# Hash attention and a SwiGLU block on one core: first loads by way of a landing room, key signs spread before the last sum, bits first in each pair's first score tile

## The chip, the core and the metric

The kernel runs on one NeuronCore of a Trainium2 chip. The engines named below work side by side and meet only at semaphores: TensorE multiplies matrices into PSUM (PE in the profile; PEld is its weight load), VectorE (DVE) and ScalarE (ACT) do elementwise work, GpSimd (POOL) sets constants and issues some DMAs, and SyncE (SP) issues most of the DMAs. ScalarE, too, issues a few at the start. Each has a queue of its own. The metric is the device time of one execution in microseconds, lower is better.

## What is computed

Attention over 4 batches, 8 heads, 768 positions and 64 features, in which a query sees only the keys with the same hash bucket, and then a SwiGLU block over the 3072 x 512 result. Cut to what matters:

```python
q_bits = (np.einsum('bhsd,dk->bhsk', q, proj) > 0)      # 6 signs for each query
k_bits = (np.einsum('bhsd,dk->bhsk', k, proj) > 0)
q_bucket = np.sum(q_bits * powers, axis=-1)             # k_bucket likewise
mask = q_bucket[:, :, :, None] == k_bucket[:, :, None, :]
scores = np.where(mask, scale * np.matmul(q, k.transpose(0, 1, 3, 2)), -1000000000.0)
attn = softmax(scores)                                  # with 1e-09 in the denominator
x = np.matmul(attn, v)                                  # -> (B*S, H*D)
g = x @ w_gate
out = (g * sigmoid(g) * (x @ w_val)) @ w_out
```

## The kernel before

**Stages.** `attention` goes through 16 pairs of heads (`pairs`, numbered 0 to 15 here), and `gated_block` then runs the SwiGLU block. Between the two, and beside both, the weights are taken apart into three parts each ("pieces": `begin_pieces` on ScalarE, `advance_pieces` with `widths` and `parts` on VectorE, loads and stores on GpSimd's queue), and attention results are split the same way (`split`, L287 to L296).

**One pair.** A pair has 12 score tiles ("units" u): two halves of 384 queries by six chunks of 128 keys, each tile for both heads. `score(u)` makes two products into the same PSUM tile: `products` multiplies transposed keys and queries in f32 (`T`) and starts the accumulation, and `mark` adds the product of the sign bits in bf16 (`bits`), which lifts matching buckets by a large number, and then has ScalarE take the exponential into a ring of weight tiles `A` (L530). After the 12 tiles, `attend` multiplies the weights with v (`av`, L545), 48 matmul records, about 7.9 us.

**Sums.** While the tiles are made, `add` sums their weights on VectorE: L563 at i = 3 and 9, L567 and L570 at i = 5 and 11. `total(n-1)` has TensorE sum the previous pair's accumulators over the partitions (L581), ScalarE copies the row out of PSUM (`fetch_row`, L586), SP moves it into `few`, VectorE inverts it (`invert`, L594), SP sends it through DRAM and back spread over the partitions, and `norm` (L610) scales the result.

**The next pair's front.** `front(n+1)` gives three steps, of which two transpose k and q on VectorE (`transpose_blocks`, L458) and stand at the head of pair n, and the third, `hash_next`, comes after the 12 tiles: four hash products (L430), then the signs of q on ScalarE (L435), the copy of the q bits to the other 32 partitions by a GpSimd DMA (`spread_q`, L447), and, handed back as a list, the signs of k and `spread_k` on VectorE (L444), which multiplies the key signs for each head. The list is worked off by `finish(rest)` after the row copy and after the last `add`.

**Order.** All order is written out by hand: `manual_schedule` leaves each engine the order of the program text. Raw k and q have one buffer each, so `load(n + 2, "qk")` on SP waits until pair n+1 is transposed. `few` stands on SP behind these eight loads.

**The start.** Pair 0 has its own path. Its q comes on SP's queue and its k on ScalarE's, in halves and by heads, four DMAs for each tensor, straight into the raw tiles [128, 6, 2, 64] (L329), so that a run of memory is 64 numbers long. `start_first` transposes them on TensorE (`tps`, L468), ScalarE evicts k (L472) and VectorE q (L475); then come the first products, the hash of all four halves, their signs and spreads, and three tiles. Ahead of it TensorE runs nine matmuls over zeros (`idle`, L367), and `hash_w` is filled from `proj` by two VectorE copies (L394).

Of the kernel before, what the change touches and what calls it, by code (L numbers as in the profile page):

```python
# [19 lines left out]
def kernel(  # L20
# [68 lines left out]
    def finish(todo):  # L89
        while todo:  # L90
            todo.pop(0)()
# [210 lines left out]
    def attention(scope):  # L302
# [9 lines left out]
        def fetch(n, name, queue, half=None):  # L312
            b, pr = pairs[n]
            if name == "v":
                t = raws["v", n] = raw.tile([P, 2, NCH, D], FP32, tag="vraw", name="vraw")
                queue.dma_start(
                    t.rearrange("p h c d -> p h (c d)"),
                    v[b, 2 * pr : 2 * pr + 2].rearrange("h (p c) d -> p h (c d)", c=NCH),
                )
                return  # L320
            src = q if name == "q" else k
            if not half:
                raws[name, n] = raw.tile([P, NCH, 2, D], FP32, tag=name + "raw", name=name + "raw",
                                         bufs=1)
            t = raws[name, n]
            if n == 0:
                cs = slice(half * CH, (half + 1) * CH)
                for h in range(2):
                    queue.dma_start(t[:, cs, h, :],  # L329
                                    src[b, 2 * pr + h].rearrange("(p c) d -> p c d", c=NCH)[:, cs, :])  # L330
                return
            blocks = t.rearrange("p c a b -> p (c a b)").rearrange(
                "p (c a d) -> p c a d", a=P // BLOCK, d=BLOCK)
            for h in range(2):
                for x in range(D // BLOCK):
                    at = h * D + x * BLOCK
                    queue.dma_start(
                        blocks[at : at + BLOCK],
                        src[b, 2 * pr + h][:, x * BLOCK : (x + 1) * BLOCK].rearrange(
                            "(a p c) d -> p c a d", c=NCH, p=BLOCK))  # L340

        def load(n, names):
            if n < len(pairs):
                for name in names:
                    fetch(n, name, nc.sync)

        two_proj = fixed.tile([P, NBITS], FP32, tag="proj", name="proj")
        for o in (0, D):
            nc.gpsimd.dma_start(two_proj[o : o + D, :], proj[:, :])
# [13 lines left out]
        for t in (sides["k", 0], sides["q", 0], sides["q", 1]):  # L363
            nc.vector.memset(t, 0.0)
        idle = two_banks("idle")
        for i in range(9):
            nc.tensor.matmul(idle[:, i % 2], zeros[:, 0:P], zeros[:, 0:512], start=True, stop=True)  # L367

        HR = 16
# [19 lines left out]

        hash_w = fixed.tile([P, BLOCK], FP32, tag="hash", name="hash")  # L390
        nc.vector.memset(hash_w, 0.0)
        for h in range(2):
            rows = slice(h * D, (h + 1) * D)
            nc.vector.tensor_copy(hash_w[rows, h * HR : h * HR + NBITS], two_proj[rows, :])  # L394
        ones = fixed.tile([P, BLOCK], FP32, tag="ones", name="ones")
        nc.gpsimd.memset(ones, 1.0)

# [5 lines left out]
            nc.gpsimd.memset(t.rearrange("p u h q -> p (u h) q")[:, :, HQ:AW], 1.0)  # L403
            twos.append(t)
        ring = [t[:, i] for t in twos for i in range(2)]

        for n, name in ((1, "k"), (1, "q"), (0, "v"), (1, "v")):
            fetch(n, name, nc.sync)
        load_words(3, nc.sync)

        T = {}
        bits = {}
# [9 lines left out]
        def front(n):  # L422
# [24 lines left out]
                nc.gpsimd.dma_start(bits["q", n][high], bits["q", n][low])  # L447

            def hash_next(todo):
                q0, q1, *ks = hash_blocks(todo)  # L450
                q0()
                q1()
                spread_q()
                return ks + [lambda: spread_k(times_k)]

            def transpose_blocks(name):
                T[name, n] = opnd.tile([P, S], FP32, tag=name + "T", name=name + "T")
                nc.vector.transpose(T[name, n], raws[name, n].rearrange("p c h d -> p (c h d)"))  # L458

            def start_first():  # L460
                for half in range(2):
                    cols = slice(half * HQ, (half + 1) * HQ)
                    for name in "kq":
# [7 lines left out]
                        if name == "k":  # L471
                            nc.scalar.activation(T[name, n][:, cols], ps[:, 0:HQ], AF.Copy,  # L472
                                                 scale=2 / OFF)
                        else:
                            nc.vector.tensor_copy(T[name, n][:, cols], ps[:, 0:HQ])  # L475

                def both_heads(sign, name, half):
                    cols = slice(half * HQ, (half + 1) * HQ)
# [33 lines left out]

        banks_of = {}

        def product(u, x, start):
            n, half, c = units[u]
            qs = slice(half * HQ, (half + 1) * HQ)
            ks = slice(c * P, (c + 1) * P)
            for h in range(2):
                rows = slice(h * D, (h + 1) * D)  # L520
                nc.tensor.matmul(banks_of[u][:, h], x["k", n][rows, ks], x["q", n][rows, qs],  # L521
                                 start=start, stop=not start)

        def products(u):
            banks_of[u] = two_banks("sc")[:, :, 0:HQ]
            product(u, T, True)

        def mark(u):
            product(u, bits, False)
            nc.scalar.activation(weights(u)[:, :, 0:HQ], banks_of.pop(u), AF.Exp,  # L530
                                 scale=SCALE * (1.0 if units[u][0] else OFF / 2))

        def score(u):
            products(u)
            mark(u)

        def attend(u):
            n, half, c = units[u]
# [84 lines left out]
                    rest.extend(f for f in steps.pop(0)() or [] if f)  # L623

        front(0)
        steps = front(1)
        last = []
        PACE = [2] * 4 + [1] * 4 + [2, 1] * 4
# [3 lines left out]
        for n in range(len(pairs)):  # L632
# [5 lines left out]
            for i in range(2 * NCH):  # L638
                if u + i > 2:
                    score(u + i)  # L640
                if n == 0 and i == TURN:
                    prepare_pair(2)
                if i % NCH:
                    add(u + i)
                if i == (2 if n else TURN):
                    load(n + 2, "qk")
            row = total(n - 1) if n else None
            if more:
                prepare_pair(1)
            if row:  # L650
                row()
            finish(rest)
            finish(last)
            while waiting:
                last.append(waiting.pop(0)())
# [277 lines left out]
```

## Time and profile before

| what | us |
|---|---|
| median of 3 runs (lowest, highest) | 913.04 (912.83, 913.85) |
| the profiled execution, device time | 913.47 |
| its span, first to last instruction | 911.4 |
| TensorE busy, attention and block | 904.0 |
| first full stream of score matmuls begins | 13.33 |
| attention's last matmul ends, block begins | 318.5 |
| one pair, score tiles to score tiles, from pair 1 on | 19.23 |

The span counts from the first to the last instruction of the program; the device time has 2.1 us more around it. A line of a timeline or of the chain in order of time starts with its start and its length in microseconds; several instructions of one kind that follow each other are merged (x4). "[0.58 <-PE joint L430]" says how long the engine had been idle before it, and what ended that. SPq, POOL DMA and ACTq lines are DMA issues, and not the transfers themselves. A chain of waits is followed backward from the last instruction: to what released it, or to the instruction before it on the same engine.

### The profile page before, as it was taken

Reading aid. Unit: us, or ns where it says so; the run is one execution under the profiler, and the core shown is the slowest. Engines: PE = TensorE matmul, PEld = TensorE weight load, DVE = VectorE, ACT = ScalarE, POOL = GpSimd, SP = SyncE. Lnnn points to the kernel's source line nnn. Section 1 sums busy time; section 2 is a strip of 40 time slices with the busy share of each in tenths; the row PEclk is TensorE's granted clock in tenths of the full one; section 3 lists DMA queues with packets and bytes.
Section 4 is the critical chain, followed back from the end, with each engine's and each line's share of the span. In section 5 each row is a group of like instructions: output and inputs, shape, how many; then the busy total and the mean of one; then the engine's idle time right before and its main releaser. Section 6 shows DMA issues by size and latency. Waiting matters only on the chain.

```text
span 911.4 us, 12610 instructions
## 1 busy us (share of the span) xinstructions
PE 904.0 (99%) x4795; PEld 636.1 (70%) x4795; DVE 666.6 (73%) x774; ACT 448.0 (49%) x604; POOL 97.0 (11%) x193
## 2 busy tenths in 40 slices
PE   8999999999999999999999999999999999999998
PEld 4444444444444488888888888888888888888886
DVE  5889999989988968779785855465668754474746
ACT  6889888878888655452414243331313233413220
POOL 1111111011111120000100000101000100001000
PEclk9999999999999999999999999999999999999999
DMA  7777788787897599685756562444434642525332
GB/s 180 132 188 199 195 214 192 162 193 208 224 227 211 200 382 331 218 289 207 297 177 238 202 259 104 173 139 157 155 139 151 242 147 97 207 70 208 104 139 93
DMA packets 145579, 174.25 MB, mean 191 GB/s; under 512 B 106496, under 2 KB 115200, under 8 KB 145520
## 3 DMA queue, kind: packets, MB, share of 16 engines
q0 software_dynamic: 22864, 116.36, 36.4%
q1 hardware_dynamic: 121056, 56.71, 24.9%
q8 instruction: 38, 0.62, 0.3%
q10 hardware_dynamic: 1600, 0.39, 0.2%
q14 instruction: 21, 0.17, 0.1%
HBM read 133.17 MB, written 39.42 MB: 189 GB/s over the span
## 4 chain that ended last, share of the span: by engine, by line
PE 97%; DVE 1%; DMA 1%; ACTq 0%; issue 0%; ACT 0%; DVEq 0%
PE a L690 29%; PE o L690 22%; PE sc L521 17%; PE n L690 14%; PE av L545 13%; PE joint L581 1%; PE joint L430 1%; DMA vraw<-in_v_dram 1%; DMA kraw<-in_k_dram 0%; DVE both L567 0%; DVE both L563 0%; DVE acc L570 0%; ACTq L329 0%; DVE kb L444 0%; DVE kT L458 0%
## 5 line engine op out<-in xcount | busy, mean ns | idle before, releaser
L690 PE MATMUL a<-xparts,ring 128*128 128x512 f32 x1152 | 273.0, 389 | 0.0
L690 PEld LDWEIGHTS a<-xparts,ring 128*128 128x128 f32 x1152 | 216.1, 188 | 45.5 <-issue 0.6
L690 PE MATMUL o<-ring,hid 128*128 128x512 f32 (+1 forms) x870 | 199.1, 388 | 0.0
L690 PEld LDWEIGHTS o<-ring,hid 128*128 128x128 f32 x870 | 162.1, 188 | 35.2 <-DVE hid L745 1.0
L521 PE MATMUL sc<-qT,kT 64*128 64x384 f32 x768 | 156.9, 487 | 0.6 <-ACT A L530 0.6
L530 ACT ACTIVATE A<-sc 128x768 f32<-128x768 f32 x192 | 151.8, 815 | 7.5 <-PE sc L521 4.2
L690 PE MATMUL n<-xparts,ring 128*128 128x512 f32 x576 | 142.2, 389 | 0.0
L545 PE MATMUL av<-A,vraw 128*64 128x386 f32 (+1 forms) x768 | 127.7, 488 | 0.0
L690 PEld LDWEIGHTS n<-xparts,ring 128*128 128x128 f32 x576 | 108.1, 188 | 22.5
L735 DVE TENSOR_TENSOR v<-v,n 128x1024 f32<-128x1024 f32 x36 | 44.0, 1221 | 98.7 <-PE n L690 98.0
L248 POOL DMA_DIRECT2D ring<-ram x108 | 56.9, 529 | 499.9 <-PE n L690 328.4
L545 PEld LDWEIGHTS av<-A,vraw 128*64 128x64 f32 x768 | 53.7, 136 | 73.3 <-issue 63.4
L521 PEld LDWEIGHTS sc<-qT,kT 64*128 64x128 f32 x768 | 67.6, 187 | 48.5 <-issue 46.3
L729 ACT ACTIVATE g<-a 128x1024 f32<-128x1024 f32 x36 | 37.0, 1027 | 130.8 <-PE a L690 126.6
L740 ACT ACTIVATE hid<-v 128x1024 fp32r<-128x1024 f32 x36 | 38.2, 1062 | 114.5 <-DVE v L739 114.5
L737 ACT ACTIVATE g<-g 128x1024 f32<-128x1024 f32 x36 | 38.2, 1062 | 86.0 <-DVE g L735 86.0
L792 DVE TENSOR_TENSOR o<-o 128x512 f32<-128x512 f32 x92 | 63.0, 687 | 20.6 <-ACT o L786 18.2
L735 DVE TENSOR_TENSOR g<-g,n 128x1024 f32<-128x1024 f32 x36 | 43.8, 1217 | 32.7 <-PE n L690 32.7
L521 PE MATMUL sc<-qb,kb 64*128 64x384 bf16 x384 | 63.4, 323 | 1.1 <-DVE kb L444 1.1
L567 DVE TENSOR_TENSOR both<-both,A 128x1536 f32<-128x1536 f32 x32 | 56.2, 1757 | 3.2
L563 DVE SCALAR_TENSOR_TENSOR both<-A 128x1536 f32<-128x1536 f32 x32 | 55.7, 1741 | 3.5 <-ACT A L530 1.9
L743 DVE SCALAR_TENSOR_TENSOR hid<-hid,v 128x1024 fp32r<-128x1024 f32 x36 | 44.0, 1224 | 19.2 <-ACT hid L740 19.1
(79 smaller groups left out, 696.8 us busy)
## 6 DMA issues: line engine op xcount, KB each, us to landing
ring<-ram POOLq DMA_DIRECT2D x108, 768.0 KB, 5.1
ram<-stage POOLq DMA_DIRECT2D x23, 768.0 KB, 5.6
ram<-stage SPq DMA_DIRECT2D x13, 768.0 KB
qraw<-in_q_dram SPq DMA_DIRECT2D x64, 96.0 KB
vraw<-in_v_dram SPq DMA_DIRECT2D x16, 384.0 KB
out_dram<-o SPq DMA_DIRECT2D x23, 256.0 KB
kraw<-in_k_dram SPq DMA_DIRECT2D x60, 96.0 KB
r<-sums SPq DMA_DIRECT2D x30, 192.0 KB
```

Of the source, the lines that this page charges most:

```text
L248: nc.gpsimd.dma_start(t.bitcast(FP32), ram[at].bitcast(FP32))
L521: nc.tensor.matmul(banks_of[u][:, h], x["k", n][rows, ks], x["q", n][rows, qs], start=start, stop=not start)
L530: nc.scalar.activation(weights(u)[:, :, 0:HQ], banks_of.pop(u), AF.Exp, scale=SCALE * (1.0 if units[u][0] else OFF / 2))
L545: nc.tensor.matmul(ps[h * D : (h + 1) * D, 0:width], raws["v", n][:, h, c, :], a[:, h, 0:width], start=c == 0, stop=c == NCH - 1)
L563: nc.vector.scalar_tensor_tensor(out=t, in0=first, scalar=S * EPS / P / 2, in1=now, op0=ALU.add, op1=ALU.add)
L567: nc.vector.tensor_tensor(t, t, now, op=ALU.add)
L690: nc.tensor.matmul(ps, w, x, start=start, stop=stop)
L735: nc.vector.tensor_tensor(two(z), two(z), n_, op=ALU.subtract)
L737: nc.scalar.activation(z, z, AF.Silu)
L740: nc.scalar.activation(h, val, AF.Copy, scale=TOWARD / STEP)
L743: nc.vector.scalar_tensor_tensor(out=l, in0=h.bitcast(FP32), scalar=-STEP, in1=val, op0=ALU.mult, op1=ALU.add)
L792: nc.vector.tensor_tensor(accs[c], accs[c], t[:, 1], op=ALU.subtract)
```

## The change

The first pair's k and q no longer land in the raw tiles. A room with the shape of the tile `both` (same buffer) takes each tensor in the order of memory, [128, head, 6, 64]; a DMA now brings one half of one tensor for both heads, in runs of 192 numbers. `start_first` begins with four copies into the raw tiles, k on ScalarE and q on VectorE, first half and second half, ahead of every eviction. One idle matmul is dropped, the filling of `hash_w` moves behind the first half's evictions, and the loads of pair 1's k and q, of two v tiles and of three weight pieces move, in the text, behind `front(0)`.

In every pair, `hash_next` hands back all six steps, the signs of k and their spread first, then the signs of q and their copy. Three of them run ahead of the last `add`, which is taken out of the loop; the others follow it, and the row copy follows all of them.

`score` makes the bits product first in each pair's first tile (u a multiple of 12), and the f32 product closes the accumulation; in all other tiles the order stays.

```diff
@@ -324,10 +324,10 @@
                                          bufs=1)
             t = raws[name, n]
             if n == 0:
-                cs = slice(half * CH, (half + 1) * CH)
-                for h in range(2):
-                    queue.dma_start(t[:, cs, h, :],
-                                    src[b, 2 * pr + h].rearrange("(p c) d -> p c d", c=NCH)[:, cs, :])
+                at = slice(half * CH * D, (half + 1) * CH * D)
+                queue.dma_start(
+                    landing[name].rearrange("p h c d -> p h (c d)")[:, :, at],
+                    src[b, 2 * pr : 2 * pr + 2].rearrange("h (p c) d -> p h (c d)", c=NCH)[:, :, at])
                 return
             blocks = t.rearrange("p c a b -> p (c a b)").rearrange(
                 "p (c a d) -> p c a d", a=P // BLOCK, d=BLOCK)
@@ -344,6 +344,9 @@
                 for name in names:
                     fetch(n, name, nc.sync)
 
+        room = att.tile([P, 2, 2, HQ], FP32, tag="both", name="landing", bufs=1)
+        landing = {name: room[:, i].rearrange("p x q -> p (x q)").rearrange(
+            "p (h c d) -> p h c d", h=2, d=D) for i, name in enumerate("qk")}
         two_proj = fixed.tile([P, NBITS], FP32, tag="proj", name="proj")
         for o in (0, D):
             nc.gpsimd.dma_start(two_proj[o : o + D, :], proj[:, :])
@@ -363,7 +366,7 @@
         for t in (sides["k", 0], sides["q", 0], sides["q", 1]):
             nc.vector.memset(t, 0.0)
         idle = two_banks("idle")
-        for i in range(9):
+        for i in range(8):
             nc.tensor.matmul(idle[:, i % 2], zeros[:, 0:P], zeros[:, 0:512], start=True, stop=True)
 
         HR = 16
@@ -389,9 +392,6 @@
 
         hash_w = fixed.tile([P, BLOCK], FP32, tag="hash", name="hash")
         nc.vector.memset(hash_w, 0.0)
-        for h in range(2):
-            rows = slice(h * D, (h + 1) * D)
-            nc.vector.tensor_copy(hash_w[rows, h * HR : h * HR + NBITS], two_proj[rows, :])
         ones = fixed.tile([P, BLOCK], FP32, tag="ones", name="ones")
         nc.gpsimd.memset(ones, 1.0)
 
@@ -404,10 +404,6 @@
             twos.append(t)
         ring = [t[:, i] for t in twos for i in range(2)]
 
-        for n, name in ((1, "k"), (1, "q"), (0, "v"), (1, "v")):
-            fetch(n, name, nc.sync)
-        load_words(3, nc.sync)
-
         T = {}
         bits = {}
 
@@ -447,17 +443,19 @@
                 nc.gpsimd.dma_start(bits["q", n][high], bits["q", n][low])
 
             def hash_next(todo):
-                q0, q1, *ks = hash_blocks(todo)
-                q0()
-                q1()
-                spread_q()
-                return ks + [lambda: spread_k(times_k)]
+                q0, q1, k0, k1 = hash_blocks(todo)
+                return [k0, k1, lambda: spread_k(times_k), q0, q1, spread_q]
 
             def transpose_blocks(name):
                 T[name, n] = opnd.tile([P, S], FP32, tag=name + "T", name=name + "T")
                 nc.vector.transpose(T[name, n], raws[name, n].rearrange("p c h d -> p (c h d)"))
 
             def start_first():
+                for half in range(2):
+                    here = slice(half * CH, (half + 1) * CH)
+                    for name, copy in (("k", nc.scalar.copy), ("q", nc.vector.tensor_copy)):
+                        copy(raws[name, n].rearrange("p c h d -> p h c d")[:, :, here],
+                             landing[name][:, :, here])
                 for half in range(2):
                     cols = slice(half * HQ, (half + 1) * HQ)
                     for name in "kq":
@@ -473,6 +471,11 @@
                                                  scale=2 / OFF)
                         else:
                             nc.vector.tensor_copy(T[name, n][:, cols], ps[:, 0:HQ])
+                    if not half:
+                        for h in range(2):
+                            rows = slice(h * D, (h + 1) * D)
+                            nc.vector.tensor_copy(hash_w[rows, h * HR : h * HR + NBITS],
+                                                  two_proj[rows, :])
 
                 def both_heads(sign, name, half):
                     cols = slice(half * HQ, (half + 1) * HQ)
@@ -512,27 +515,34 @@
 
         banks_of = {}
 
-        def product(u, x, start):
+        def product(u, x, start, stop):
             n, half, c = units[u]
             qs = slice(half * HQ, (half + 1) * HQ)
             ks = slice(c * P, (c + 1) * P)
             for h in range(2):
                 rows = slice(h * D, (h + 1) * D)
                 nc.tensor.matmul(banks_of[u][:, h], x["k", n][rows, ks], x["q", n][rows, qs],
-                                 start=start, stop=not start)
+                                 start=start, stop=stop)
 
         def products(u):
             banks_of[u] = two_banks("sc")[:, :, 0:HQ]
-            product(u, T, True)
-
-        def mark(u):
-            product(u, bits, False)
+            product(u, T, True, False)
+
+        def mark(u, last=True):
+            if last:
+                product(u, bits, False, True)
             nc.scalar.activation(weights(u)[:, :, 0:HQ], banks_of.pop(u), AF.Exp,
                                  scale=SCALE * (1.0 if units[u][0] else OFF / 2))
 
         def score(u):
-            products(u)
-            mark(u)
+            if u % (2 * NCH):
+                products(u)
+                mark(u)
+            else:
+                banks_of[u] = two_banks("sc")[:, :, 0:HQ]
+                product(u, bits, True, False)
+                product(u, T, False, True)
+                mark(u, False)
 
         def attend(u):
             n, half, c = units[u]
@@ -623,6 +633,9 @@
                     rest.extend(f for f in steps.pop(0)() or [] if f)
 
         front(0)
+        for n, name in ((1, "k"), (1, "q"), (0, "v"), (1, "v")):
+            fetch(n, name, nc.sync)
+        load_words(3, nc.sync)
         steps = front(1)
         last = []
         PACE = [2] * 4 + [1] * 4 + [2, 1] * 4
@@ -640,16 +653,20 @@
                     score(u + i)
                 if n == 0 and i == TURN:
                     prepare_pair(2)
-                if i % NCH:
+                if i % NCH and i < 2 * NCH - 1:
                     add(u + i)
                 if i == (2 if n else TURN):
                     load(n + 2, "qk")
             row = total(n - 1) if n else None
             if more:
                 prepare_pair(1)
+            for _ in range(3):
+                if rest:
+                    rest.pop(0)()
+            add(u + 2 * NCH - 1)
+            finish(rest)
             if row:
                 row()
-            finish(rest)
             finish(last)
             while waiting:
                 last.append(waiting.pop(0)())
```

## The prediction

> **What bounds the kernel now.** I read the page's busy line, then the chain of waits, then the chain in order of time for the first 125 us.
>
> ```profile
> PE 904.0 (99%) x4795; PEld 636.1 (70%) x4795; DVE 666.6 (73%) x774; ACT 448.0 (49%) x604; POOL 97.0 (11%) x193
> ...
> PE 97%; DVE 1%; DMA 1%; ACTq 0%; issue 0%; ACT 0%; DVEq 0%
> ```
>
> TensorE sets the end, and its matmuls are not made fewer. Only three things can be won: the start, stalls, and bubbles between stages. The chain in order of time shows the first two:
>
> ```profile
> 2.37 4.12 DMA kraw<-in_k_dram
> 6.49 0.14 issue
> 6.62 0.85 PE tps L468 x6
> 7.47 0.84 PE sc L521 x4
> 8.32 0.78 PE joint L430 x8
> ...
> 13.33 6.88 PE sc L521 x50
> ...
> 106.50 0.42 DVE kb L444
> 106.94 0.42 DVE kb L444
> 107.36 0.14 issue
> 107.50 9.22 PE sc L521 x68
> ```
>
> The start waits for the last landing of k, at 2.37 + 4.12 = 6.49; from there to the hash (8.25 in the timeline) is 1.76, and from 13.33 on TensorE runs through. At 107.50 it waited for key signs (kb, L444) that VectorE reached late. The timelines of single engines show the rest:
>
> ```profile
> 28.83 0.92 PE L521 MATMUL sc<-qT,kT 64*128 64x384 f32 x4
> 29.58 0.33 PE L521 MATMUL sc<-qb,kb 64*128 64x384 bf16 x2
> 29.74 0.81 PE L521 MATMUL sc<-qT,kT 64*128 64x384 f32 x4
> ...
> 40.29 1.16 ACT L435 ACTIVATE qb<-joint,columns 32x384 bf16<-32x384 f32 x2 [0.58 <-PE joint L430]
> 41.47 0.48 ACT L586 COPY row<-joint 128x384 f32<-128x384 f32 x1
> 41.97 1.18 ACT L435 ACTIVATE kb<-joint,columns 32x384 bf16<-32x384 f32 x2
> ...
> 45.20 0.23 DVE L594 RECIPROCAL few<-few 128x12 f32<-128x12 f32 x1 [1.17 <-DMA few<-row]
> ...
> 96.18 0.93 DVE L458 STREAM_TRANSPOSE qT<-qraw 128x768 f32<-128x768 f32 x1
> ...
> 119.66 0.52 POOL L447 DMA_DIRECT2D qb<-qb  x1 [3.62 <-ACT qb L435]
> ```
>
> The first f32 product after the attention stage takes 0.92, the next 0.81: a bubble of 0.11. The rows of 40 to 45 are a second loop: row copy, `few` out on SP, reciprocal, weight pieces, the next pair's transposes, SP's loads, `few` again. The transposes end at 53.56, 74.88, 97.11 and 116.42; the hashes that need them start at 58.62, 77.85, 97.16 and 117.3. So this loop is slower than TensorE up to the fourth pair, catches it at 97.16, and is left behind again afterwards. What it gains or loses in pair 1 arrives at TensorE there.
>
> **The start.** Eight loads with 256-byte runs become four with 768-byte runs. The windows of 2 to 6 us show the DMA engines 0.85, 1.16, 1.09 and 0.76 busy, so packets set the landing. By the trace's packet records 256 bytes take 18 ns and 1024 bytes 46 ns; on that line 768 bytes take 37. Before: 3072 x 18 / 16 = 3.5 us, really 1.86 to 5.85. After: 1024 x 37 / 16 = 2.4 us, with the same slack 2.7, so 1.86 to 4.6, plus 0.4 to 0.6 to the semaphore: the second halves land at 5.0 (bounds 4.7 to 5.6, where issue or receipt holds them).
>
> Added are four copies. ScalarE: 128x384 as L472, 0.49. VectorE: between 0.35 (L153 does 512 elements out of SBUF in 0.42) and 0.56 (L475, out of PSUM); 0.35 taken, and it doesn't decide. The first k copy runs about 4.0 to 4.5, so transposes start near 4.75. The first eviction on ScalarE queues behind the second k copy (5.02 to 5.51) and runs to 6.0; the second transposes start at 5.65 and end by 6.25; products run 6.44 to 7.29. `hash_w`'s two copies (0.17 each) now stand behind the first q eviction on VectorE (5.65 to 6.2), so the second q eviction runs 6.6 to 7.16, just ahead of the hash at 7.29. **Start: -0.95**, bounds -0.35 and -1.25. The path beyond the hash is unchanged. The moved loads keep their order on SP, where none of the start's instructions stands among them; their first waited for the k transposes (issue at 7.18) and comes with these. The landing room is needed again at 15.60 (L563), ten us later.
>
> One idle matmul less: they start 0.43 apart (nine from 1.32, 4.00 us), so eight end by 4.9 and nothing waits for the ninth. Against this speaks the Trainium skill, "TensorE: Matmul & The Clock Gate", "What's actually happening": the clock is released after a busy window of about 3.4 us that is not tied to the kernel's start. Eight times 0.43 is 3.4, no margin. By the rows the sum keeps -0.95; by the rule a missed window leaves products and hash (0.84 + 0.78) at half rate, up to +1.6. One case in ten, as transposes follow at once.
>
> **The row copy moves back.** On ScalarE the order q, q, row, k, k becomes k, k, q, q, row. In pair 1 `few` leaves at 41.97, right behind the row. New: 41.97 - 0.95 - 0.10 (bits first, below) + 1.16 = 42.08. It landed 3.2 later there; in the next pairs issue to reciprocal is 2.2 (64.31 to 66.51, 84.91 to 87.09). I take 2.2: reciprocal at 44.28 instead of 45.20, **-0.92**; with 3.2 again it is +0.1. VectorE is no earlier: its L563 of 38.12 ends at 38.84 shifted, it then waits for the k signs until 40.43 (cover gone, 1.6 idle), spreads (0.85), sums (1.76 + 0.96) and is free at 44.1. In pair 2 that wait is under 0.4 and lies inside the 1.79 idle before 66.51. From pair 3 on VectorE comes later than the signs, and spread ahead of sum costs it nothing. In later pairs `few` stands behind SP's k loads (81.62 + 3.19, then 84.91), so the later row is hidden.
>
> **Pair 4.** Transposes end at 97.11 - 0.92 = 96.19, hash at 96.24. TensorE alone would be there at 97.08 - 0.95 - 4 x 0.10 = 95.7, so 0.5 of the gain is lost in this wait. **Key signs ahead of the sum:** the spread of 106.50 moves in front of L567 and L570 (103.64 to 106.46), 2.8 us; the first bits product was due 0.75 after its scores began (105.85), at 106.60, and came at 107.50: **-0.90**. What is late next is pair 5's hash: 117.32 - 0.92 - 0.90 - 0.10 = 115.40, while its transposes come at 116.42 - 0.92 = 115.50. So -1.77 there.
>
> **Query bits come later.** Behind the k signs the POOL copy of q bits starts 1.16 later, and bits first needs it 0.75 sooner. The trace's issue to landing is 2.1 to 5.3, median 3.6. From its start the attention stage leaves 7.91; issue stands at 1.58, now 2.74, so 5.17 is allowed. Only pair 5 (119.66, 5.3) exceeds it: +0.15. POOL's following transfers wait for VectorE anyway.
>
> **Bits first.** The f32 product's bubble of 0.11 falls away; a bits product after a wait shows 0.34 against 0.33, so 0.01 remains: 0.10 per pair. The same page's section "LDWEIGHTS (loading the stationary operand)" prices a load by columns alone, 128 / 1.2 = 107 ns whatever the type; by that the swap would bring nothing but the fast load for non-f32 weights, about 0.05. The row decides: weight loads of 64x128 are 187 ns in f32, 93 in bf16. Fifteen pairs have such a tile; the first five are already in the sums above, the ten from pair 6 on give **-1.0** (by the rule -0.5).
>
> **Sum.** -1.77 + 0.15 - 1.0 = -2.6 on the profiled execution (913.47, span 911.4): 910.9. The median of the runs shown is 913.04, and part of these 0.43 may be the 3.2 us landing, which other executions need not share; without it the kernel before gains by itself. I therefore add 0.2: **911.1**.
>
> **Rivals.**
> - *The loop eats the start* (0.25). The `few` landing stays at 3.2, or second halves land at 5.6: -2.6 + 0.6 to 1.0, and against a median without that landing about -1.3: 911.5 to 912.2. For it: the reciprocal waits 1.17 for `few` in the trace. Against: 2.2 in the pairs after.
> - *Query bits late in every pair* (0.12), the slower side. If 1.16 later puts the copy into SP's loads each time, as at 99.53 (4.9) and 119.66 (5.3), TensorE stops at the first tile of each pair. It decides from a landing of 5.17 on; at 5.7, 0.5 x 14 = 7 us, less 2.6: 917. Against: twelve of fifteen take 4.3 or less.
> - *The clock comes a window later* (0.08): +1.0 to 1.6, 912 to 912.5.
> - *More than forecast* (0.10): landing at 4.7 and no wait at 96.2: 909.6 to 910.2.
> - The forecast itself, 910.3 to 911.6: 0.45.
>
> A difference under 0.2% (1.83 us, 911.21 to 914.87) can't be told from none. Faster: 0.40 of the forecast's 0.45, all of the 0.10, 0.06 of the loop's: 0.56. Slower: 0.12, and 0.01 for what I overlook. Within: 0.31. The range 909.6 to 913.0 covers all but the slower case and some of the tail.
>
> **What would show it.** k's second half lands near 5.0 and TensorE runs through from about 12.4; the reciprocal of pair 1 stands near 44.3; the wait for kb at 107.5 is gone; VectorE idles 1.6 ahead of the first spreads only; the first f32 product after attention reads 0.81, fifteen times. Wrong would be: waits on q bits at several pair starts, a hash near 97.2 or later, or a start above 13.

## The result and the profile after

| what | before | after |
|---|---|---|
| median of 13 runs each, us (lowest, highest) | 912.75 (912.07, 913.85) | 911.12 (910.13, 911.90) |
| the profiled execution, device time | 913.47 | 910.18 |
| its span | 911.4 | 908.4 |
| first hash of the start (the L430 product of 8.25, now L426) | 8.25 | 7.46 |
| reciprocal of pair 1 | 45.20 | 44.29 |
| hash of pair 4 | 97.16 | 95.91 |
| hash of pair 5 | 117.32 | 115.14 |
| attention's last matmul ends, block begins | 318.49 | 315.31 |
| one pair, score tiles to score tiles (most pairs) | 19.23 | 19.13 |

The hash of pair 4 is the one behind pair 4's score tiles; it makes the signs for pair 5, so a wait for these shows at pair 5's first tile. Three pairs of before were longer than the others: 19.34 (pair 4), 20.13 (pair 5) and 19.31 (pair 6). After the change only pair 5 is, with 19.26.

Changed over unchanged time is 0.9982, with a 95% interval of 0.9973 to 0.9990: 1.6 us less. The same kernel run again beside the experiments (e4 below) gave 910.58 against 913.08, 0.9975 (0.9966 to 0.9985), 2.5 us less. The profiled execution of before was near the top of that kernel's runs, the one of after near the bottom of its own, so the two traces differ by 3.3: 3.18 less in attention, 0.22 more in the block, and 0.33 less around the span. This last part is no chance of the two traces: in all executions measured beside the experiments the unchanged kernel has 2.06 to 2.17 around its span, the changed one (e4) 1.74 to 1.83. No view shows what lies there. So about 0.3 of each median's gain lies outside the span, and by the medians the span fell by about 1.3 and 2.2.

The busy line and the chain of waits of the page of after:

```profile
PE 902.2 (99%) x4794; PEld 634.8 (70%) x4794; DVE 666.1 (73%) x776; ACT 449.9 (50%) x606; POOL 97.0 (11%) x193
...
PE 99%; DVE 0%; ACT 0%; issue 0%; DVEq 0%
```

The DMA share of the chain is gone, and VectorE's too. TensorE's busy time fell by 1.8 with one matmul less (0.4); the other 1.4 are about the fifteen bubbles of 0.1, which stand in the busy time of before. The chain in order of time of after, first 125 us (start, length, what):

```profile
4.92 1.76 PE tps L466 x12
6.68 0.85 PE sc L524 x4
7.53 0.78 PE joint L426 x8
8.31 2.05 PE sc L524 x10
...
10.38 0.81 ACT A L534
...
12.53 6.88 PE sc L524 x50
...
95.31 0.78 PE joint L591 x8
96.09 0.65 PE joint L426 x8
96.73 7.91 PE av L555 x48
104.64 9.80 PE sc L524 x72
114.44 0.78 PE joint L591 x8
115.22 0.76 PE joint L426 x8
115.99 7.91 PE av L555 x48
```

It no longer has a landing in it: the transposes follow the idle matmuls at 4.92. At 10.38 one exponential stands on the path ahead of pair 0's last key signs; from 12.53 on the chain stays on TensorE. Where it stood at 106.5 on `kb` before, the score stage of pair 5 now runs through as one piece of 72. Only the hash of pair 5 is longer than its neighbours (0.76 for 0.65): it waited about 0.1 for its transposes. The timelines of single engines of after (start, length; in brackets the idle time before and what ended it):

```profile
4.10 0.51 ACT L457 COPY kraw<-landing 128x384 f32<-128x384 f32 x1 [1.02 <-DMA landing<-in_k_dram]
5.24 0.51 ACT L457 COPY kraw<-landing 128x384 f32<-128x384 f32 x1 [0.63 <-DMA landing<-in_k_dram]
...
28.04 0.34 PE L524 MATMUL sc<-qb,kb 64*128 64x384 bf16 x2
28.21 1.45 PE L524 MATMUL sc<-qT,kT 64*128 64x384 f32 x8
...
40.61 0.85 DVE L440 TENSOR_SCALAR kb<-kb,columns 32x768 bf16<-32x768 bf16 x2 [1.61 <-ACT kb L431]
...
44.29 0.23 DVE L604 RECIPROCAL few<-few 128x12 f32<-128x12 f32 x1 [0.17 <-DMA few<-row]
...
52.68 6.59 SPq L337 DMA_DIRECT2D qraw<-in_q_dram  x4
59.32 2.78 SPq L337 DMA_DIRECT2D kraw<-in_k_dram  x4
62.19 0.59 SPq L598 DMA_DIRECT2D few<-row  x1
```

The second half of k lands at 5.22 (0.02 ahead of its copy). The bits product now comes straight after the attention stage with no bubble. VectorE idles 1.61 ahead of its spread in pair 1, and the reciprocal follows at 44.29. The last three lines are SP in pair 2; they read against the same timeline of before:

```profile
53.59 7.81 SPq L337 DMA_DIRECT2D qraw<-in_q_dram  x4
61.45 2.77 SPq L337 DMA_DIRECT2D kraw<-in_k_dram  x4
64.31 0.60 SPq L588 DMA_DIRECT2D few<-row  x1
```

SP began 0.91 earlier, as the earlier reciprocal lets it, and the four q loads took 6.59 to issue instead of 7.81, so `few` left 2.12 earlier. The transposes that pair 4's hash needs therefore end at 95.02 instead of 97.11, and TensorE doesn't wait for them.

### The profile page after: what moved, and what is told of

It is laid out like the page before. It is cut to its first block, busy times and chain, and to the rows that moved or that the text cites. A ratio compares the mean times of both kernels' runs of the same rounds, so it can differ in the third digit from the quotient of the medians.

```text
span 908.4 us, 12579 instructions
## 1 busy us (share of the span) xinstructions
PE 902.2 (99%) x4794; PEld 634.8 (70%) x4794; DVE 666.1 (73%) x776; ACT 449.9 (50%) x606; POOL 97.0 (11%) x193
## 4 chain that ended last, share of the span: by engine, by line
PE 99%; DVE 0%; ACT 0%; issue 0%; DVEq 0%
PE a L707 29%; PE o L707 22%; PE sc L524 17%; PE n L707 14%; PE av L555 14%; PE joint L591 1%; PE joint L426 1%; PE idle L370 0%; PE tps L466 0%; ACT A L534 0%; DVE kb L440 0%; ACT kb L431 0%; DVE o L833 0%; DVE kb L365 0%; DVEq L945 0%
## 5 line engine op out<-in xcount | busy, mean ns | idle before, releaser
L524 PE MATMUL sc<-qT,kT 64*128 64x384 f32 x768 | 152.9, 483 | 0.6 <-ACT A L534 0.6
```

## The experiments

The theory: three separate gains (start, key signs, bubbles) that add up. The rivals: the loop over `few` and SP's loads eats the start; the late query bits cost; the clock is released late. Each ratio is to executions of before on the same chip, measured beside the experiment; their medians are 913.08 us for e1 to e4, 912.31 for e5 to e8, 912.95 for e9 to e12.

**e1 to e3: each part alone.** In e1 only the loads, the landing room, the four copies, the moved filling and the eight idle matmuls are taken over; order and products stay as before:

```diff
-        for i in range(9):
+        for i in range(8):
...
+                    for name, copy in (("k", nc.scalar.copy), ("q", nc.vector.tensor_copy)):
+                        copy(raws[name, n].rearrange("p c h d -> p h c d")[:, :, here],
+                             landing[name][:, :, here])
```

> Only the first pair's loads are changed (landing room, four copies, eight idle matmuls, moved loads); order of signs and products as before. My theory: parts add up; the stream of score matmuls starts near 12.5 instead of 13.33, nothing in pair 1 moves the row back, so the reciprocal of pair 1 and the hash of pair 4 come 0.8 earlier too, the wait for key signs at pair 5 (0.9) stays: 0.8 us faster. Rival: VectorE's loop takes the start away again (its transposes for pair 4 stay at 97.1, a new wait at that hash): 0 to 0.2 faster.

Measured: 911.99 (0.9990, 0.9981 to 0.9999). In its profile the first hash comes at 7.84, 0.41 earlier than before, and attention ends at 317.83, 0.66 earlier. So the loop takes nothing of this start away: the hash of pair 4 no longer waits (0.11 before), and the waits for key signs, 0.91 in pair 5 and 0.08 in pair 6 before, are 0.45 and 0.39. The reciprocal of pair 1 comes even earlier than in the changed kernel (44.29), because under the old order VectorE doesn't idle ahead of it:

```profile
43.65 0.23 DVE L600 RECIPROCAL few<-few 128x12 f32<-128x12 f32 x1
```

e2 takes over the order alone:

```diff
-                q0, q1, *ks = hash_blocks(todo)
...
+                return [k0, k1, lambda: spread_k(times_k), q0, q1, spread_q]
...
+            add(u + 2 * NCH - 1)
+            finish(rest)
             if row:
                 row()
-            finish(rest)
```

> Only the order after the last tile is changed (key signs first, their spread ahead of the last sum, query signs and the row copy behind). My theory: the wait for key signs at pair 5 (0.9) goes, the reciprocal of pair 1 stays near 45.3 since the later row is made up by a landing of 2.2, hash of pair 4 near 97.2: 0.8 to 0.9 us faster. Rival: the later row holds up the loop, reciprocal of pair 1 at 46.3, hash of pair 4 at 98.3, and query bits land after pair 5's tiles could begin: 0 to 0.3 slower.

Measured: 912.00 (0.9991, 0.9982 to 1.0000). Every pair of its profile takes 19.23, so the stall of 107.5 is gone with this part by itself, and no pair waits for query bits. Attention ends at 317.24, 1.25 earlier than before. Of this, 0.17 is an earlier first hash (8.08), which this edit doesn't touch; 1.1 is the order's.

e3 takes over the products alone:

```diff
-            products(u)
-            mark(u)
+            if u % (2 * NCH):
...
+                product(u, bits, True, False)
+                product(u, T, False, True)
+                mark(u, False)
```

> Only the first tile of each pair is changed (bits product first). My theory: each pair's stage of tiles is 0.10 shorter (9.86 instead of 9.96), 15 times 1.5 less, but the wait for key signs at pair 5 loses the f32 product that covered 0.65 of it and TensorE arrives earlier at hash 4: 0.5 to 0.9 us faster in all. Rival: the bubble between attention and the next tiles doesn't go with the type of the weights, stages stay at 9.96, and only the lost cover remains: 0.6 slower.

Measured: 911.94 (0.9991, 0.9983 to 1.0000). Its runs lie from 911.28 to 914.00, and the profiled one is the slowest of them. Its timelines show why the bits must not come first without the order (first tile of pair 5):

```profile
105.41 0.85 DVE L444 TENSOR_SCALAR kb<-kb,columns 32x768 bf16<-32x768 bf16 x2
...
106.41 0.34 PE L521 MATMUL sc<-qb,kb 64*128 64x384 bf16 x2 [1.00 <-ACT xT L559]
106.58 1.47 PE L521 MATMUL sc<-qT,kT 64*128 64x384 f32 x8
```

TensorE stood idle for 1.00 before this product. The view names a ScalarE copy that ended last, but that copy (`xT`) is no operand of it; the spread of the signs is, and it ended at 106.26, 0.15 before. The same wait, at the first tiles of pairs 5, 6, 10 and 12, adds up to 3.05 in this execution (from first tile to first tile), while each pair without it takes 19.13 or 19.14.

**e4: the changed kernel again**, beside the three.

> The changed kernel once more, unchanged, to see what differs between its executions (910.1 to 911.9). My theory: the start and the 0.10 per pair are the same in each; an execution near 911.5 shows a longer wait at SP for its loads in pair 2 or 3 (few out later than 62.2 and 83.1) and TensorE waiting 0.5 to 1 for the transposes of pair 4 or 5. Rival: the difference lies in the start (landing or clock release), with the stream beginning at 13 or later, and no wait at the hashes.

Measured: 910.58 (0.9975, 0.9966 to 0.9985), 910.08 to 912.26. The medians of the three parts alone gain 1.1 each, 3.3 together, against 2.5; with intervals of about 0.8 on each side that is no disagreement. A part of the excess lies outside the span, where the gains don't add: 0.24 in e1, 0.33 in e2, none in e3, but 0.32 in e4. In its profile the first hash comes at 7.74, no hash waits, and all pairs take 19.13 or 19.14. Its runs of 911.5 and above were not the profiled ones, so what they lost isn't seen.

**e5: everything but the order.**

```diff
-                return [k0, k1, lambda: spread_k(times_k), q0, q1, spread_q]
+                q0()
+                q1()
+                spread_q()
+                return ks + [lambda: spread_k(times_k)]
```

> The changed kernel with the old order after the last tile (query signs, row copy, key signs, all behind the last sum); loads and bits first stay. My theory: bits first needs the earlier key signs, so TensorE now waits for them at the first tile of several pairs (about 1 at pair 5, tenths in later ones, up to 4 us in the worst executions): 0.8 to 1.5 us slower than the changed kernel, 911.4 to 912.1. Rival: the parts only add, and the order is worth the 1.08 that it brought alone, all of it at pair 5, with no wait for key signs elsewhere.

Measured: 912.01 (0.9995, 0.9987 to 1.0004): without the order nothing of the change can be told from before, and 0.25 of the 0.30 between the medians lies outside the span. TensorE's waits in its profile (what waited for what: total, times, longest):

```profile
PE sc L527 <- DVE kb L440: 1.9, 3, 0.9
```

One of the three is the start's; the other two stand at the first tiles of pairs 5 and 6, 0.67 and 0.96 by the distance from the first tile of the pair before. Attention ends at 317.23, 1.92 later than in the changed kernel: 1.63 of these two waits, and 0.40 of a later first hash in this execution, less the 0.1 at pair 5's hash. So in these traces the order is worth about 1.5 in the changed kernel and 1.1 alone (e2). A reason would be that bits first needs the signs 0.75 earlier.

**e6: the row copy ahead of the query signs.** If its later place cost the loop, this would give it back.

```diff
-            finish(rest)
             if row:
                 row()
+            finish(rest)
```

> The changed kernel with the row copy between the key signs and the query signs. My theory: the row copy is not on the path (in pair 1 VectorE was idle only 0.17 before its reciprocal, later the few transfer stands behind SP's loads), query bits start 0.5 later and still land in time: within 0.3 us of the changed kernel, pair 1's few leaves near 41.2, its reciprocal stays near 44.1. Rival: the later row holds VectorE's loop, so its reciprocals of pairs 1 to 4 come 0.5 to 1.1 earlier: 0.3 to 0.6 faster; or query bits are late and TensorE waits at first tiles: slower by 0.3 or more.

Measured: 910.42 (0.9976, 0.9967 to 0.9985). `few` leaves at 41.33 in pair 1 instead of 42.30, and the reciprocal comes at 44.27 for 44.29:

```profile
44.27 0.22 DVE L604 RECIPROCAL few<-few 128x12 f32<-128x12 f32 x1
```

No idle time stands ahead of it any more, so VectorE isn't free before. Counted from the first hash, which comes 0.23 later here (7.69), the reciprocal is 0.25 earlier; all pairs take 19.13 or 19.14, so nothing of that reaches the end. The late row costs nothing. What delays the reciprocal against e1 (43.65) and e5 (43.51) is the new order on VectorE, with its 1.6 of idle time ahead of the key signs.

**e7 and e11: short runs into the same room.** What does the order of memory bring, with copies in both cases?

```diff
-                at = slice(half * CH * D, (half + 1) * CH * D)
...
+                for h in range(2):
+                    queue.dma_start(landing[name][:, h, cs, :],
...
-            "p (h c d) -> p h c d", h=2, d=D) for i, name in enumerate("qk")}
+            "p (c h d) -> p h c d", h=2, d=D) for i, name in enumerate("qk")}
```

> The changed kernel with its landing room laid out like the raw tile, so that the first loads are eight DMAs in 256-byte runs again and the four copies stay. My theory: run length sets the landing; the second halves land at 6.3 to 6.5 as in the kernel before, the copies add 0.5, the hash comes near 8.8 (7.5 in the changed kernel): 1.3 us slower. Rival: the landing is set by issue and receipt, not by packets, and the hash stays below 8: 0 to 0.4 slower.

Measured: 912.81 (1.0005, 0.9996 to 1.0014), and a first hash at 10.46: a miss of 1.7, by two things that I had not expected. Its timelines:

```profile
4.64 1.28 ACT L457 ACT_TABLE_LOAD   x1 [4.64 <-DMA landing<-in_k_dram]
5.93 0.93 ACT L457 COPY kraw<-landing 128x384 f32<-128x384 f32 x2
...
6.59 0.87 PE L466 MATMUL tps<-ident,kraw 128*128 128x128 f32 x3 [1.67 <-ACT kraw L457]
7.25 0.85 PE L466 MATMUL tps<-ident,qraw 128*128 128x128 f32 x3
```

The first copy waits for two transfers here instead of one, and ScalarE's table load, which runs at 1.79 in the changed kernel, comes only after that wait; it sits on the path with 1.28. TensorE stands still from 4.92 to 6.59, and its transposes then take 0.85 for three where they took 0.49. So e7 measures three costs at once; e6, measured beside it, gave 910.42. e11 is e7 with a copy of one number on ScalarE first, which pulls the table load ahead:

```diff
+        early = fixed.tile([1, 2], FP32, tag="early", name="early")
+        nc.gpsimd.memset(early, 0.0)
+        nc.scalar.copy(early[:, 1:2], early[:, 0:1])
```

> The first loads in eight DMAs with 256-byte runs into a landing room, as before in this study, but with one small ScalarE copy ahead of everything, so that the table load (1.28, which had moved behind the wait for the landing) is out of the way. My theory: second halves land near 6.1, hash near 8.4 with the clock released in time, so 0.9 to 1.0 later than in the changed kernel: 911.5. Rival: TensorE stays at half rate in the gap between idle matmuls and transposes, and the hash comes at 9 or later.

Its timelines:

```profile
2.91 1.28 ACT L360 ACT_TABLE_LOAD   x1 [2.91 <-issue]
...
6.24 0.51 ACT L460 COPY kraw<-landing 128x384 f32<-128x384 f32 x1 [0.97 <-DMA landing<-in_k_dram]
...
8.45 0.51 PE L429 MATMUL joint<-kT,hash 128*32 128x384 f32 x1
```

The table is loaded before the landing, the transposes run at full rate (0.49), and the second half of k comes 1.00 later than with long runs (6.24 for 5.24), the hash 0.99 later (8.45 for 7.46). That is what the order of memory brings at the start. It is the packets and not the number of issues: e11's last issue ends at 2.88, its last packet of 256 bytes at 5.59 (768 bytes: 4.74), with the DMA engines busy at 1.04, 1.06 and 1.30 from 2 to 5 us. In the median it can hardly be seen: 911.05 (0.9984, 0.9975 to 0.9993), 0.3 above the 910.78 of e12 beside it. Where the rest of the 0.99 went in the other executions no run shows; the profiled one, at 911.74, lost another 0.85 in pair 4.

**e8: key signs of pair 0 earlier.** That exponential of 10.38 stands ahead of the key signs of pair 0's second half. e8 puts these signs first:

```diff
+                both_heads(signs[2], *todo[2])
                 for i in range(3):
                     mark(i)
-                    if i < 2:
-                        both_heads(signs[2 + i], *todo[2 + i])
+                    if i == 1:
+                        both_heads(signs[3], *todo[3])
```

> The changed kernel with the key signs of pair 0's second half put ahead of the first exponential on ScalarE (it idles 0.78 there), the query signs of that half after the second. My theory: the spread that TensorE waits for at 12.53 is done by 11.0, so the unbroken stream begins about 0.4 earlier: 0.4 faster than the changed kernel, first stage of attention near 19.7 instead of 20.12. Rival: ScalarE's exponentials bound this stretch and attention begins at the same time: no change.

Measured: 910.45 (0.9975, 0.9964 to 0.9985), the ratio of e4; e6 beside it gave 910.42. The first attention stage begins at 19.57 instead of 20.12, but attention ends at 315.56, no earlier than in the changed kernel (315.31). The time is lost in pair 5, as TensorE's timeline of e8 shows:

```profile
104.13 0.69 PE L525 MATMUL sc<-qb,kb 64*128 64x384 bf16 x2
104.51 1.60 PE L525 MATMUL sc<-qT,kT 64*128 64x384 f32 x8
...
115.38 0.52 PE L426 MATMUL joint<-qT,hash 128*32 128x384 f32 x2 [0.24 <-DVE qT L451]
```

The two bits products of the first tile take 0.69 together where they took 0.34 at 28.04 of the changed kernel. The records of the two heads start at 104.13 and 104.50: the second head's query bits, which POOL copies, landed at 104.46. This is the slower rival's wait, 0.38 long, once in fifteen pairs. It is no idle time in the view, since the first head's product covers it. At the other end of the score tiles the hash stands 11.25 after the first product instead of 10.46; less the 0.38, some 0.4 is a wait for the transposes (they end at 115.32), of which the view shows 0.24. So the loop eats the earlier start here, and the query bits take their share.

**e9 and e10: `few` off SP's queue.** If the loop is late because `few` is issued behind SP's loads, issuing it elsewhere should give its hashes slack, and e8's gain should then reach the end.

```diff
-                nc.sync.dma_start(few, row.rearrange("(g r) t -> r g t", r=BLOCK)[0])
+                nc.scalar.dma_start(few, row.rearrange("(g r) t -> r g t", r=BLOCK)[0])
```

> The changed kernel with the few transfer issued from ScalarE's queue, right behind the row copy, instead of SP's, where it stands behind eight loads of q and k. My theory: what is left of the start's gain is lost in VectorE's loop (row, few, reciprocal, pieces, transposes, SP's loads, few); with few out of that loop the idle times ahead of the reciprocal (0.2 to 1.2 in pairs 2 to 5) go, transposes of pairs 4 and 5 end a microsecond or more before their hashes, and the slow executions (911 to 912.3) go: median 910.2 to 910.5, spread under 1 us. Rival: the slow executions come from the start, and the spread stays 2 us; or ScalarE's 0.6 for the issue is felt in the exponentials and the time rises by 0.5 or more.

In the timelines of after, pair 3, SP issues its k loads until 82.6 and `few` then:

```profile
83.06 0.59 SPq L598 DMA_DIRECT2D few<-row  x1
85.00 0.23 DVE L604 RECIPROCAL few<-few 128x12 f32<-128x12 f32 x1 [0.99 <-DMA few<-row]
```

and in those of e9:

```profile
80.58 0.53 ACTq L598 DMA_DIRECT2D few<-row  x1
...
83.94 0.22 DVE L604 RECIPROCAL few<-few 128x12 f32<-128x12 f32 x1
```

The reciprocal waits no more. The transposes for pair 5's hash end at 114.20 instead of 115.08, 0.85 ahead of the hash. Since the changed kernel lost only 0.1 there, the median says nothing by itself: 910.55 (0.9972, 0.9962 to 0.9982). Its spread is under 1 us, as expected. e10 adds the edit of e8:

> The same with the key signs of pair 0's second half ahead of the first exponential. My theory: the 0.5 to 0.8 that this won at the start (attention from 19.57 instead of 20.1 to 20.4) and lost again at the hashes of pairs 4 and 5 (0.1 and 0.8) now arrives at the end: 0.4 to 0.6 faster than the one before it, 909.6 to 909.9. Rival: another bound takes it (query bits, VectorE's own work in pairs 3 to 5), and it equals the one before it within 0.2.

Measured: **909.87** (0.9967, 0.9955 to 0.9980), 909.56 to 910.02 over five runs. All pairs take 19.13 or 19.14 from a start of 19.57, and attention ends at 314.64. What e8 lost is there. At the first tile of pair 5 the bits products take 0.34 again (0.69 in e8):

```profile
104.02 0.34 PE L525 MATMUL sc<-qb,kb 64*128 64x384 bf16 x2
```

The transposes for pair 5's hash end at 113.65, 0.83 ahead of it, and the query bits of pair 4 landed at 102.62 (104.46 in e8), so both of e8's waits went together and this edit doesn't separate them. The median is 3.1 below before. All five runs are below all eight of e9 (910.14 to 910.93) beside them: with `few` off SP's queue, e8's edit is worth 0.7; with `few` on it, the medians of e8 and e6 show nothing.

**e12: nine idle matmuls in the changed kernel** (`range(8)` to `range(9)`), to see whether the eighth is enough for the clock.

> The changed kernel with nine idle matmuls as before. My theory: the ninth ends at 5.3, the first transposes begin 0.4 later, but the second half's copy (5.24 to 5.75) sets the rest: hash within 0.2 of 7.46 to 7.7, time within 0.2 us of the changed kernel. Rival: eight idle matmuls leave no margin for the clock's release, some executions of the changed kernel run products and hash at half rate, and nine make the slow executions rarer: 0.4 faster in the median.

Measured: 910.78 (0.9976, 0.9967 to 0.9985). TensorE's timeline of e12:

```profile
5.14 0.85 PE L466 MATMUL tps<-ident,kraw 128*128 128x128 f32 x3
5.78 0.63 PE L466 MATMUL tps<-ident,qraw 128*128 128x128 f32 x3
6.25 0.49 PE L466 MATMUL tps<-ident,kraw 128*128 128x128 f32 x3
```

In spite of the ninth the first transposes run at nearly half rate, and the hash comes at 8.00, later than expected (7.9 at most). With eight, the first three took 0.77 in the changed kernel, and in e1 nine of them were slow (0.85, 0.85, 0.75). In e4 full rate came before the idle matmuls had ended, which took 3.28 for 3.60:

```profile
1.32 3.28 PE L370 MATMUL idle<-kb 128*128 128x512 bf16 x8 [1.32 <-DVE kb L365]
4.70 0.52 PE L466 MATMUL tps<-ident,kraw 128*128 128x128 f32 x3
```

So full rate begins between about 4.1 (e4) and 6.5 (e1) in these executions, with nine at about 5.2 (before) to 6.0 (e12); only e7 is later still. It costs up to 0.4 at the hash (7.84 in e1, 7.46 in the changed kernel), and eight or nine isn't what decides. The Trainium skill, "TensorE: Matmul & The Clock Gate", "What's actually happening", has the activity window run freely, so that the transition moves by about 0.5 us either way with its phase; the spread of 2.4 seen here fits that in kind and is more than twice as wide. No run sets the phase, so it stays an explanation.

## Why the prediction was right, point by point

Forecast were 911.1 and a gain of about 0.2%; measured were 911.12 and, again, 910.58. The forecast gave 0.56 to a gain of more than 0.2%, and the two comparisons fall on either side of that (0.18% and 0.25%). Direction and size are right; that the number is so close is luck, as the steps show:

- **Start, -0.95 forecast, -0.79 measured, and about -0.5 on average.** The two traces are the best pair on record: the three with the old start have their first hash at 8.08 to 8.25 (mean 8.18), the eight with the new start and eight idle matmuls at 7.46 to 7.86 (mean 7.64; e7 and e11 left out). So this term was mis-sized, within the bounds that the forecast gave. The 768-byte packets took 36 ns in the median (37 forecast), and the second half of k landed at 5.22 instead of 5.0. Transposes, evictions and products queue as written: second transposes at 5.80 (5.65), hash at 7.46 (7.29). e11 shows that the runs' length carries it: 0.99 at the hash. The four copies cost about 0.2 of that, by which e11, with copies and short runs, is behind before (8.45 for 8.25).
- **Clock.** One case in ten was kept for a missed release, which would hold products and hash at half rate. In no profile of the changed kernel does it: only some transposes are slow, in kernels with nine idle matmuls too (e3, e12), at most 0.4 at the hash. The forecast took the window's length from the rule and left out its moving phase, so a loss of 0 to 0.4 in each execution should have stood in place of one of 1.6 in every tenth. e7, with 1.67 idle ahead of the transposes, shows the missed release itself.
- **Reciprocal of pair 1, 44.28 forecast, 44.29 measured,** with VectorE's 1.6 of idle time (1.61); `few` landed inside the 2.2 that was chosen over 3.2. The match to 0.01 is luck: `few` left at 42.30 (42.08 forecast) and came within 1.99. In pair 2 VectorE idled 0.66 for the signs (under 0.4 forecast). e6 confirms the other half of the step, that VectorE isn't free earlier.
- **Pair 4, the step that failed in size.** The gain of 0.92 was carried through the loop unchanged, to transposes at 96.19 and a wait of 0.5. They ended at 95.02. The term left out is SP's issue time of the q loads in pair 2, which was taken as fixed and shrank by 1.2 (6.59 for 7.81). The earlier begin isn't the cause: in e1 and e5 the loads begin earlier still (52.03, 51.90) and take 7.90 and 7.78, in e2 they begin at 53.44 and take 6.84. The four kernels with the old order take 7.5 to 7.9, the ten with the new one 6.5 to 7.9; what sets it was not tested. In e11, where it is longest, pair 4's hash waits for its transposes.
- **Key signs, -0.90: right.** No wait at any pair's first tile from pair 1 on, in e2 none either, and in e5 and e3 it returns at pairs 5 and 6, larger in sum, as 0.67 and 0.96, or 1.07 and 1.27. That bits first makes this order necessary was said only in the 0.75 of the sum.
- **Pair 5 limited by its transposes:** forecast 115.50, measured 115.08, with the hash right behind at 115.14. The step stands in kind; it is 0.4 earlier by what pair 4 brought.
- **Query bits, +0.15 forecast, 0 measured.** By the landing records the bits copied in pairs 4 and 5 were there 0.55 and 0.78 ahead of the next pair's first tile, all others at least 1.45. The margin is thin at these two places, and in e8, where the bits of pair 4 were due 0.45 earlier and landed 0.43 later, the product waited 0.38. So the mechanism of the slower rival exists, but where it can happen in one pair or two, not in fourteen.
- **Bits first, 0.10 a pair: measured 19.23 to 19.13 or 19.14.** From the hash of pair 5 to the end of attention the gain grew by 1.00 (2.18 to 3.18), 0.08 of it a short wait of before in pair 6: the row of the trace was right, and not the 0.5 that the prediction had by the rule. Why the bubble goes is inferred from the load times of the weights (187 and 93 ns); no run changes these alone.
- **The sum.** Forecast -2.62 of the span, measured -2.96 between the two traces: 0.41 more at pair 5's hash (2.18 for 1.77), 0.15 of query bits that weren't lost, less 0.22 by which the block took longer. By the medians the span fell by only 1.3 and 2.2.
- **The 0.2 for the median.** It stands for a shorter landing in other executions of before, and no run showed it as such. Against it stands the 0.33 outside the span, for which the sum has no term. 911.1 met the first median (911.12) and missed the second by 0.5: the changed kernel's own runs spread over 910.1 to 912.3, which the sum has nothing for. So the match to 0.02 is luck; the right size is not.

The rival that *the loop eats the start* was the right second: it is what happens in e8 (0.4 at the hash of pair 5) and e11 (0.85 at the hash of pair 4), though not in e1. In the profiled changed kernel it just doesn't bite, with 0.9 to spare at pair 4 and 0.1 missing at pair 5.

Open is what the upper runs of the changed kernel (911.4 to 912.3) lose; none of them was profiled. A late `few` would fit, and e9's eight runs end at 910.93. But those of e6 and e12, which leave `few` on SP, end at 911.00 and 911.27, so e9 doesn't show it.

## What to carry to other kernels

A start that is made earlier is worth only what the slower loop behind it lets through (e8 against e10): follow the gain to the place where that loop catches the bounding engine, and look at the issue times of its queue as well as at its instructions. Opening an accumulation with the product whose weights load faster removed a bubble of 0.1 at every change of stage here, but it makes that product's operands due earlier, so the order that produces them belongs to the same edit. Where a small transfer that an engine waits for is issued behind bulk loads, another queue gives the slack that later edits need.

## What the runs showed of the hardware, unexpected

- ScalarE's table load (1.28 us) ran at 1.79 where the first instruction of that engine waits for one transfer, and after the landing, at 4.64, where it waits for two (e7); that the number is the reason was not tested apart. An instruction without such a wait ahead of it brought it to 2.91 (e11).
- The start of TensorE's full rate moved by up to 2.4 us between executions of nearly the same work, more than I had expected (the first three transposes took 0.52 to 0.87). With 1.67 us idle after the idle matmuls (e7) all twelve took 0.85 to 0.87 for three; with gaps of 0.49 and 0.54 (e11) they kept 0.49 to 0.55.
- A wait of one matmul behind another of the same group needn't appear as idle time: e8's 0.38 shows only as a longer pair of products.
- The issue of the same four loads on SP's queue took 6.50 to 7.93 us in the same place of the fourteen traces, and doesn't follow the time at which it began.
- A part of the gain, 0.33 of 2.10 us, lies outside the span of first to last instruction, in every execution; the order brings it (e2), the start most of it too (e1: 0.24), the bits product none (e3).
